# One exponential for both score tiles of a pair, in a top-32 attention and highway layer on one core

## The chip, the cores and the metric

The kernel runs on one core of one Trainium2 chip. The metric is the device time of one execution in microseconds. The core's engines are TensorE (PE, with its weight loads PEld), VectorE (DVE), ScalarE (ACT), GpSimd (POOL) and SyncE (SP), which here only issues DMAs. Each engine works through its own queue in order; what crosses from one engine to another waits on semaphores.

## The reference

```
q, k, v: (8, 8, 576, 64) f32, normal * 0.1
scores = q @ k.T / sqrt(64)
kth    = 32nd largest score of each row
attn   = exp(scores - rowmax) where scores >= kth, else 0
attn   = attn / (sum(attn) + 1e-9)
x      = (attn @ v), heads side by side: (4608, 512)
H = relu(x @ w_h);  T = sigmoid(x @ w_t + b_t)
out    = T * H + (1 - T) * x
```

## The kernel before

The work is cut into units. For each of the 8 batches there are 4 full query tiles (qt 0 to 3, 128 rows) times 8 heads, one unit each, and a rest of 64 rows (qt 4), where one unit holds two heads on the two halves of the partitions. Two units that follow each other are a pair: 18 pairs for a batch, 16 of them of full tiles, 144 pairs in all, of which 128 are of full tiles. A score tile of a unit is 128 x 576.

The main loop calls `step(i)` once for each pair, and each step works on several pairs at once. The order in which `step` writes the instructions is the order of each engine's queue (a manual schedule). In the words of one step:

- PE adds the masks of pair i to its scores in PSUM (`mask_add`, L410), then makes the attention values of pair i-3 (`values`, L494), then some filler matmuls (`spare`, L278), then the scores of pair i+2 (`scores`, L309, L318; L326 and L335 for the rest rows). After that come pieces of the layer behind the attention or of the transposes of the next batch (L522, L250).
- DVE finds candidates in the scores of pair i+1 (`segments`, 12 instructions on L353), then the largest masked scores of pair i (`below`, L420, two instructions), then goes through `refine` of pair i+1 (L366 to L382; the last one, L382, gives the row maximum and the threshold). In between it picks the kth value of pair i (`hits` L426, `pick_b` L439) and makes the masked exponentials of pair i-1 (`keep_min` L450 for the first unit, `keep_mul` L460 for the second, both on two bf16 tiles in SBUF).
- ACT makes a step function of the scores of pair i-1 (`above`, L443), evacuates one piece for the layer or the transposes, copies the values to SBUF in every second step (`xs_copy`, L508), and then does the exponential of the first unit of pair i (`expo`, L416), the copy of both score tiles of pair i+1 from PSUM (`copy_scores`, L348, one instruction of 1152 columns), possibly an evacuation of a transpose, the exponential of the second unit, and the two mask instructions of pair i+1 (`mask_count`, L397), which wait for L382.
- POOL makes the step function of the second unit (`above_one`, L454), one or two elementwise pieces of the layer (`pool_work`: L564, L610, L611, L624), multiplies hits (`pick_a`, L436), issues at most a DMA or two, and then makes the two biases (`biases`, L391) for the next step: the row maxima times -scale for the exponentials (`tb`) and the kth values times a large constant for `above` (`eb`). A dependency written by hand (`after`) holds `biases` until DVE's second masked exponential (`keep_mul`) has ended.

The masked exponentials are turned by DMA (`transposes`, L481) and multiplied with `v`, whose extra column holds a constant, so that the sum of each row comes out as a 65th column. When all 8 heads of a query tile are there, `ffn_pieces` divides by the sums (`norm`, L557, L559) and runs the layer in pieces over the next steps.

Behind the last pair `finish` does the end of the pipeline in an order of its own, and a check: ACT's Sign instructions with accumulators (`sure`, L934) count rows on which the short way is sound, and if the count is not full, a second, general pass (`tc.If(fine < 1)`) computes everything again.

Of the kernel before, what the change touches and what calls it, by code (L numbers as in the profile page):

```python
# [9 lines left out]
AF = mybir.ActivationFunctionType  # L10
ALU = mybir.AluOpType
FP32 = mybir.dt.float32
BF16 = mybir.dt.bfloat16
# [13 lines left out]
def kernel(  # L27
# [44 lines left out]
    kqpool = ctx.enter_context(tc.tile_pool(name="kq", bufs=2))  # L72
    scpool = ctx.enter_context(tc.tile_pool(name="sc", bufs=5))
    gpool = ctx.enter_context(tc.tile_pool(name="g", bufs=2))
    epool = ctx.enter_context(tc.tile_pool(name="e", bufs=4))
    cpool = ctx.enter_context(tc.tile_pool(name="c", bufs=4))
    etpool = ctx.enter_context(tc.tile_pool(name="et", bufs=6))
    xpool = ctx.enter_context(tc.tile_pool(name="x", bufs=3))
# [28 lines left out]
    for i in range(NE):  # L107
        en = consts.tile([P, 2, 2, 16], FP32, name=f"en{i}")
        nc.vector.memset(en[:, 0, :, 0:1], 3.0e38)
        ends.append(en)  # L110
    csum = consts.tile([P, NU], FP32)
    nc.vector.memset(wall[:, 0:2, KTH : KTH + 1], 0.0)

    def kth(u):
# [2 lines left out]
    def tb(u):  # L117
        return be[:, u // 2, u % 2, 0:1]
# [16 lines left out]
    vbs = []  # L135
    for i in range(2):
        vb = consts.tile([P, H, nck, DE], BF16, name=f"vb{i}")
        nc.gpsimd.memset(vb[:, :, :, D:DE], 1.0)
        vbs.append(vb)
    NEP = 4  # L140
    eps_sb = []
# [204 lines left out]
    def copy_scores(both):  # L346
        sc = scpool.tile([P, 2, S], FP32, name="sc")
        nc.scalar.copy(sc[:], both)  # L348
        return [sc[:, s, :] for s in range(2)]

    def segments(cand, sc, lo, hi):
        for s in range(lo, hi):
# [5 lines left out]
    def refine(g, cand):  # L358
# [28 lines left out]
        )  # L387
        yield

    def biases(g):  # L390
        return nc.gpsimd.tensor_tensor(be[:, g], wall[:, 2 * g : 2 * g + 2, TOP : KTH + 1 : KTH - TOP], fac[:], ALU.mult)  # L391


# [13 lines left out]
    def mask_add(ps, m1, s):  # L407
        cuts = ((0, MAIN), (MAIN, S)) if s == 0 else ((0, rem), (rem, S))
        for s0, s1 in cuts:
            nc.tensor.matmul(  # L410
                ps[:, s0:s1], ident_b[:], m1[:, s0:s1], start=False, stop=True, skip_group_check=True
            )

    def expo(u, sc):
        e = epool.tile([P, S], BF16, name="e")
        nc.scalar.activation(e[:], sc, AF.Exp, bias=tb(u), scale=scale)  # L416
        return e

    def below(u, ps):
# [19 lines left out]
        nc.vector.tensor_reduce(wall[:, pair[0] + 2 : pair[0] + 4, KTH], hit[:], mybir.AxisListType.X, ALU.add)  # L439

    def above(u, sc):
        r = epool.tile([P, S], BF16, name="r")
        nc.scalar.activation(r[:], sc, AF.Relu, bias=eb(u), scale=BIGK)  # L443
        return r

# [4 lines left out]
        return ep, nc.vector.tensor_tensor(ep[:, pad : pad + S], e[:], r[:], ALU.min)  # L450

    def above_one(u, sc):
        r = epool.tile([P, S], BF16, name="ro")
        nc.gpsimd.tensor_scalar(r[:], sc, kth(u), None, ALU.is_ge)  # L454
        return r

# [5 lines left out]
    def keep(u, sc, e):  # L462
        ep = eps_sb[u % NEP]
        pad = (u % 2) * (SP - S)
        return ep, nc.vector.scalar_tensor_tensor(
            out=ep[:, pad : pad + S],
            in0=sc,
            scalar=kth(u),
            in1=e[:],
            op0=ALU.is_ge,  # L470
            op1=ALU.mult,
        )
# [73 lines left out]

    blocks = []

    def ffn_pieces(b, qt, xs):
        nh, ng, w = shape_of(qt)  # L550
        st = dict(b=b, qt=qt, xs=xs)
        blocks.append(st)

        def norm():
            xs3 = xs[:, 0 : nh * DE].rearrange("p (h e) -> p h e", e=DE)
            rinv = cpool.tile([P, H], FP32, name="rinv")
            nc.vector.tensor_scalar(rinv[:, 0:nh], xs3[:, :, D], 1e-9, 2.0, ALU.add, ALU.mult)  # L557
            yield
            nc.vector.reciprocal(rinv[:, 0:nh], rinv[:, 0:nh])  # L559
            x = xpool.tile([P, dm], FP32, name="x")  # L560
            st["x"] = x
# [12 lines left out]

            pool_work.append((scaled, w))
            yield

        by_dma = isinstance(b, int) and units[-1][0:2] > (b, qt + 2)

        def cast():  # L580
            xb = xpool.tile([P, dm], BF16, name="xb")
            nc.gpsimd.dma_start(xb[:, 0:w], st["x"][:, 0:w])
            return partial(turn, xb)

        def turn(xb):
            st["xT"] = fpool.tile([P, n_g, P], BF16, name="xT")
            nc.sync.dma_start_transpose(st["xT"][:, 0:ng, :], xb[:, 0:w])
            flying.append(b)
            ready.extend([hh, tt])

        def xt():
            ps = fps.tile([P, 512], FP32, tag="fp", name="fp")
            for g in range(ng):
                nc.tensor.transpose(ps[:, g * P : (g + 1) * P], st["x"][:, g * P : (g + 1) * P], ident_f[:])
            xT = fpool.tile([P, n_g, P], BF16, name="xT")
            st["xT"] = xT
            psv = ps[:].rearrange("p (g j) -> p g j", j=P)
            return lambda: nc.scalar.copy(xT[:, 0:ng, :], psv[:, 0:ng, :])

        def hh():  # L600
            ps = fps.tile([P, 512], FP32, tag="fp", name="fp")
            project(ps, qt, st["xT"], wh, False)
            h2 = hpool.tile([P, dm], FP32, name="h2")
            s1 = xpool.tile([P, dm], FP32, name="s1")
            st["h2"], st["s1"] = h2, s1
            x = st["x"]

            def evac():
                nc.scalar.activation(h2[:, 0:w], ps[:, 0:w], AF.Relu)
                pool_work.append((lambda e: e.tensor_add(s1[:, 0:w], h2[:, 0:w], x[:, 0:w]), w))  # L610
                pool_work.append((lambda e: e.tensor_sub(h2[:, 0:w], h2[:, 0:w], x[:, 0:w]), w))  # L611

            return evac

        def tt():
            ps = fps.tile([P, 512], FP32, tag="fp", name="fp")
            project(ps, qt, st["xT"], wt, True)
            if by_dma:
                flying.pop()
            t = fpool.tile([P, dm], FP32, name="tt")  # L620
            h2, s1 = st["h2"], st["s1"]

            def gated(e):
# [12 lines left out]
            return evac  # L636

        return norm

    def blk_norm(k):  # L640
# [4 lines left out]
        nc.vector.tensor_scalar(rinv[:, 0:nh], xs3[:, :, D], 1e-9, 2.0, ALU.add, ALU.mult)  # L645
# [77 lines left out]
    def start_scores(g):  # L723
        b = units[pairs[g][0]][0]
        for u in pairs[g]:
            for h in units[u][2]:
                ensure_prep(b, h // 2)
        st[g] = dict(ps=scores(pairs[g], preps[b]), sc=[None, None], et=[None, None], e=[None, None])
        st[g]["seg"] = 0
        st[g]["cand"] = cands[g % len(cands)]  # L730

# [23 lines left out]
    def back_xs(g):  # L755
# [6 lines left out]
        po.clear()  # L762
        po.update(t=pso_tile(), n=0)
        if units[pairs[g][1]][2][-1] == H - 1:
            norms.append(ffn_pieces(b, qt, xs_t[b, qt]))

    late = []
    kind = [False]

    def masks_of(g):  # L770
        pr = pairs[g]
# [3 lines left out]
    def step(i):  # L775
# [40 lines left out]
            below(pr[0], st[i]["ps"][0])  # L816
            below(pr[1], st[i]["ps"][1])
        if live:
            st[i]["e"] = [expo(pr[0], st[i]["sc"][0])]
        if nxt:  # L820
            copy_both(i + 1)
        if ev:
# [10 lines left out]
                late.append(piece)  # L833
        spare(4 if late else 10)
        if live:
            st[i]["e"].append(expo(pr[1], st[i]["sc"][1]))
            pass
        ra = refine(i + 1, st[i + 1]["cand"]) if nxt else iter(())

# [83 lines left out]

    cond = consts.tile([P, NU], FP32)
    signs = consts.tile([P, NU], BF16)
    cnt = consts.tile([P, 3], FP32)
    edge = consts.tile([P, 3], FP32)
    for j, e in enumerate((-(2.0**-60), 2.0**26, -(2.0**-100))):
        nc.vector.memset(edge[:, j : j + 1], e)
    flag = consts.tile([1, 1], I32)  # L930

# [11 lines left out]
    def finish():  # L943
# [7 lines left out]
        def xs_of(qt, h0, n):  # L951
# [4 lines left out]
            return dict(b=B - 1, qt=qt, xs=xs_t[B - 1, qt])  # L956

        def masked(unit, s, of):
            return keep(unit[s], of["sc"][s], of["e"][s])
# [22 lines left out]
        mask_add(cur["ps"][1], cur["m"][1], 1)  # L982
        project(zh, z["qt"], z["xT"], wh, False)
        below(pr[1], cur["ps"][1])
        es = [expo(u, cur["sc"][s]) for s, u in enumerate(pr)]
        cur["e"] = es
        x1 = xps.tile([P, 3 * BANK], FP32, tag="x", name="xs")
        project(bank(x1, 1), z["qt"], z["xT"], wt, True)
        blk_gate(z, bank(x1, 1))
# [16 lines left out]
            nc.scalar.copy(cur["et"][s][:].rearrange("p c q -> p (c q)"), turned)  # L1006
        sure(0, wall[:, 2 : NU + 2, KTH], 1.0)
        sure(1, wall[:, 0:NU, TOP], -1.0)
        values_of(i - 1, 0)
        blk_norm(ya)  # L1010
        blk_xt(ya, bank(x1, 2))
# [22 lines left out]
        nc.vector.tensor_scalar(flag[:], po["t"][0:1, 0:1], 3.0 * P * NU - 0.5, None, ALU.is_ge)  # L1034
        blk_diff(yb, bank(x2, 0))
        return blk_out(yb)

# [101 lines left out]
```

## Time and profile before

| | |
|---|---|
| time, median of 3 runs | 806.49 us (806.15 to 808.53) |
| profiled execution, its own time | 806.17 us |
| its span in the trace | 804.5 us |
| busy: DVE | 772.8 us (96%) |
| busy: ACT | 757.2 us (94%) |
| busy: PE | 686.7 us (85%) |
| busy: POOL | 559.9 us (70%) |
| mean granted TensorE clock | 0.996 |

Busy time is the union of an engine's instructions, each with its start-up and its tail. The instructions of one engine overlap: the next one starts before the tail of the last has ended. So what an instruction costs in a full queue is the distance from its start to the start of the next one, and that is less than its duration.

### The profile page before, as it was taken

The numbers are of one execution on the slowest core, as the hardware profiler recorded it, in microseconds if no ns is written. First come the engines' busy times: TensorE is split into PE (matmuls) and PEld (weight loads), VectorE is DVE, ScalarE is ACT, GpSimd is POOL, SyncE is SP. The second block draws the span as 40 slices with busy tenths as digits, with TensorE's granted clock in tenths as the row PEclk, the third lists the DMA queues.
The fourth block names the chain that finished last, engine by engine and source line by source line (L and its number), as shares of the span: only waits on it lengthen the run. The fifth ranks groups of instructions, "written<-read, shape, count | busy, mean of one in ns | idle before, by whom it ended". The sixth has DMA issues, their size and how long they took to land.

```text
span 804.5 us, 20583 instructions
## 1 busy us (share of the span) xinstructions
PE 686.7 (85%) x6369; PEld 494.7 (61%) x6459; DVE 772.8 (96%) x4020; ACT 757.2 (94%) x1401; POOL 559.9 (70%) x712
## 2 busy tenths in 40 slices
PE   7889998888888888888987889888888888988884
PEld 5666766566666666566665666666666566665662
DVE  5999999999999999999999999999999999999996
ACT  5999999999999999999999999999999999999984
POOL 2666867777777767777767776777776777766750
PEclk9999999999999999999999999999999999999998
DMA  6789968996799667998669766898767996555653
GB/s 121 87 137 159 134 116 140 141 143 93 140 152 148 108 96 137 154 131 125 102 135 159 125 113 107 150 156 126 112 121 136 160 124 109 90 106 110 108 90 88
DMA packets 346359, 100.37 MB, mean 125 GB/s; under 512 B 330624, under 2 KB 338432, under 8 KB 346240
## 3 DMA queue, kind: packets, MB, share of 16 engines
q1 hardware_dynamic: 291024, 79.16, 54.1%
q0 software_dynamic: 53536, 19.34, 22.6%
q8 instruction: 53, 0.87, 0.4%
q10 hardware_dynamic: 1680, 0.46, 0.3%
q14 instruction: 66, 0.54, 0.2%
HBM read 31.72 MB, written 9.44 MB: 51 GB/s over the span
## 4 chain that ended last, share of the span: by engine, by line
ACT 37%; DVE 32%; PE 23%; DMA 4%; issue 3%; SPq 1%; another core or an unknown queue 0%; DVEq 0%; ACTq 0%
ACT m L397 15%; DVE wall L420 12%; DVE cand L353 9%; ACT e L416 7%; ACT sc L348 6%; PE pso L278 5%; ACT r L443 4%; PE xs L309 4%; PE xs L326 3%; DVE ep L450 3%; DMA xT<-xb 3%; PE fp L522 3%; PE xs L410 3%; PE pso L494 2%; ACT xs L508 2%
## 5 line engine op out<-in xcount | busy, mean ns | idle before, releaser
L353 DVE MAX8 cand<-xs 128x8 f32<-128x96 f32 x1728 | 297.5, 248 | 11.4 <-PE xs L335 6.2
L278 PE MATMUL pso<-cst,ident_b 128*128 128x252 bf16 x1841 | 246.8, 272 | 42.8 <-ACT xs L508 40.4
L454 POOL TENSOR_SCALAR ro<-sc,wall 128x576 bf16<-128x576 f32 x135 | 232.8, 1724 | 0.0
L416 ACT ACTIVATE e<-sc,be 128x576 bf16<-128x576 f32 x288 | 226.5, 787 | 0.1
L278 PEld LDWEIGHTS <-ident_b 128*128 128x128 bf16 x1841 | 173.4, 98 | 81.4 <-issue 49.5
L420 DVE MAX8 wall<-xs 128x8 f32<-128x576 f32 x288 | 204.3, 751 | 5.6 <-PE xs L410 3.5
L309 PE MATMUL xs<-kT,qT 64*128 64x256 f32 x1024 | 145.3, 400 | 30.6 <-DVE high L366 26.2
L348 ACT COPY sc<-xs 128x1152 f32<-128x1152 f32 x144 | 161.0, 1118 | 0.7 <-DVE cand L353 0.6
L309 PEld LDWEIGHTS xs<-kT,qT 64*128 64x128 f32 x1024 | 93.0, 186 | 61.3 <-issue 37.6
L397 ACT ACTIVATE m<-xs,wall 128x576 int8<-128x576 f32 x144 | 107.4, 746 | 18.2 <-DVE wall L382 17.1
L436 POOL TENSOR_TENSOR hit<-hit,wall 128x18 f32<-128x18 f32 x143 | 32.4, 227 | 121.2 <-DVE hit L426 114.0
L397 ACT ACTIVATE m<-sc,wall 128x576 int8<-128x576 f32 x144 | 111.4, 773 | 0.0
L443 ACT ACTIVATE r<-sc,be 128x576 bf16<-128x576 f32 x143 | 109.9, 769 | 0.0
L410 PE MATMUL xs<-m,ident_b 128*128 128x512 bf16 (+1 forms) x512 | 92.7, 274 | 17.3 <-ACT m L397 15.2
L494 PEld LDWEIGHTS <-et 128*128 128x128 bf16 (+1 forms) x1600 | 68.6, 100 | 19.2 <-issue 3.5
L391 POOL TENSOR_TENSOR be<-wall,fac 128x4 f32<-128x4 f32 x144 | 29.2, 203 | 72.5 <-DVE ep L460 53.7
L410 PEld LDWEIGHTS <-ident_b 128*128 128x128 bf16 x576 | 51.7, 97 | 44.8 <-issue 24.1
L494 PE MATMUL pso<-vb,et 128*128 128x65 bf16 (+1 forms) x1600 | 74.4, 194 | 4.2 <-DMA et<-ep 0.3
L450 DVE TENSOR_TENSOR ep<-e,r 128x576 bf16<-128x576 bf16 x143 | 64.6, 452 | 0.2 <-ACT r L443 0.2
L318 PEld LDWEIGHTS xs<-kd,qT 128*128 128x128 f32 x256 | 38.1, 188 | 42.5 <-issue 42.1
L318 PE MATMUL xs<-kd,qT 128*128 128x128 f32 x256 | 62.5, 326 | 0.0
L460 DVE TENSOR_TENSOR ep<-e,ro 128x576 bf16<-128x576 bf16 x135 | 60.7, 449 | 0.0
(127 smaller groups left out, 1028.9 us busy)
## 6 DMA issues: line engine op xcount, KB each, us to landing
kin<-in_k_dram SPq DMA_DIRECT2D x64, 128.0 KB, 2.9
qin<-in_q_dram SPq DMA_DIRECT2D x62, 128.0 KB, 3.1
out_dram<-s SPq DMA_DIRECT2D x30, 256.0 KB, 2.8
s<-h POOLq DMA_DIRECT2D x29, 256.0 KB, 4.0
et<-ep SPq DMA_TRANSPOSE x286, 3.3
xb<-x POOLq DMA_DIRECT2D x30, 128.0 KB, 3.0
vb<-in_v_dram POOLq DMA_DIRECT2D x28, 128.0 KB, 4.8
vb<-in_v_dram POOLq DMA_DIRECT2D x24, 64.0 KB, 3.1
```

Source lines behind the costliest of these rows:

```text
L278: nc.tensor.matmul(po["t"][:, 4 * DE : BANK], ident_b[:], cst[:, 0 : BANK - 4 * DE], start=True, stop=True, skip_group_check=True,)
L309: nc.tensor.matmul(ps[:, mo + n0 : mo + n0 + 256], qT[r : r + D, hp, qs : qs + P], kT[r : r + D, hp, n0 : n0 + 256], start=(n0 == 0), stop ...
L318: nc.tensor.matmul(ends, qT[:, hp, qs : qs + P], kd[:, hp, :], start=True, stop=True)
L348: nc.scalar.copy(sc[:], both)
L353: nc.vector.max(cand[:, s, :], sc[:, s * SEG : (s + 1) * SEG])
L397: nc.scalar.activation(m1[:].bitcast(I8)[:, 1 : 2 * S : 2], ps, AF.Sign, bias=wall[:, u, THR : THR + 1], scale=ABOVE, accum_out=csum[:, u ...
L410: nc.tensor.matmul(ps[:, s0:s1], ident_b[:], m1[:, s0:s1], start=False, stop=True, skip_group_check=True)
L416: nc.scalar.activation(e[:], sc, AF.Exp, bias=tb(u), scale=scale)
L420: nc.vector.max(wall[:, u, THR + 1 : KTH], ps)
L443: nc.scalar.activation(r[:], sc, AF.Relu, bias=eb(u), scale=BIGK)
L454: nc.gpsimd.tensor_scalar(r[:], sc, kth(u), None, ALU.is_ge)
L494: nc.tensor.matmul(pso[r0 : r0 + ql, col : col + DE], ets[s][:, c, gi * P2 : gi * P2 + ql], vb[:, h, vc, :], start=(c == 0), stop=(c == nc ...
```

## The change

For pairs of full tiles, ACT does one exponential over both score tiles (1152 columns) instead of two over 576. The bias of one instruction is the same for both halves of a row, so both units are measured from the larger of the two row maxima. The exponential stands where the first one stood, ahead of the copy of the next scores; the place of the second one stays empty. Pairs of the rest rows go on with two instructions, now both at the first place.

What goes with it:

- `biases` of such a pair becomes two POOL instructions: the kth value of the first unit times the constant, and the larger of two maxima times -scale. The hand-written dependency on `keep_mul` holds the one that is returned, the second.
- The small constant that is added to a sum must be in the measure of that unit. For each full query tile (32 in all) `distances` computes, on DVE, the distance of each head's own maximum to that of its pair, and on ACT the exponential of it (128 x 8). `denominators` then multiplies by it (a `scalar_tensor_tensor` in place of a `tensor_scalar`). The extra column of `v` holds 2 instead of 1, which takes the place of the factor 2.
- A fourth `sure` counts the rows whose two maxima are less than 40 apart (in the exponent); if one is not, the general pass runs.
- The tiles of the exponentials hold a pair each: 2 buffers of 1152 columns instead of 4 of 576.

```diff
-    epool = ctx.enter_context(tc.tile_pool(name="e", bufs=4))
+    epool = ctx.enter_context(tc.tile_pool(name="e", bufs=2))
...
+    dist = consts.tile([P, NU], FP32)
+    nc.gpsimd.memset(dist[:], 0.0)
...
-        nc.gpsimd.memset(vb[:, :, :, D:DE], 1.0)
+        nc.gpsimd.memset(vb[:, :, :, D:DE], 2.0)
...
-        return [sc[:, s, :] for s in range(2)]
+        return [sc[:, s, :] for s in range(2)] + [sc[:]]
...
+    def joint(g):
+        return units[pairs[g][0]][1] < nfull
+
     def biases(g):
+
+        if joint(g):
+            top = wall[:, 2 * g : 2 * g + 2, TOP]
+            nc.gpsimd.tensor_scalar(be[:, g, 0, 1:2], wall[:, 2 * g, KTH : KTH + 1], -BIGK * (1.0 - 2.0**-24), None, ALU.mult)
+            return nc.gpsimd.tensor_scalar(be[:, g, 0, 0:1], top[:, 0:1], top[:, 1:2], -scale, ALU.max, ALU.mult)
         return nc.gpsimd.tensor_tensor(be[:, g], wall[:, 2 * g : 2 * g + 2, TOP : KTH + 1 : KTH - TOP], fac[:], ALU.mult)
...
+    def expo_both(g, both):
+        e = epool.tile([P, 2, S], BF16, name="e")
+        nc.scalar.activation(e[:], both, AF.Exp, bias=be[:, g, 0, 0:1], scale=scale)
+        return [e[:, s, :] for s in range(2)]
...
+    def distances(g):
+
+        u0, u1 = pairs[g][0] + 2 - H, pairs[g][0] + 2
+        nc.vector.scalar_tensor_tensor(
+            out=dist[:, u0:u1].rearrange("p (g s) -> p g s", s=2),
+            in0=wall[:, u0:u1, TOP].rearrange("p (g s) -> p g s", s=2),
+            scalar=scale,
+            in1=be[:, g + 1 - NP : g + 1, 0, 0].unsqueeze(2).to_broadcast([P, NP, 2]),
+            op0=ALU.mult,
+            op1=ALU.add,
+        )
+        low = cpool.tile([P, H], FP32, name="share")
+        nc.scalar.activation(low[:], dist[:, u0:u1], AF.Exp)
+        return low
+
+    def denominators(rinv, sums, share):
+
+        if share is None:
+            return nc.vector.tensor_scalar(rinv, sums, 2.0e-9, None, ALU.add)
+        return nc.vector.scalar_tensor_tensor(
+            out=rinv, in0=share[:], scalar=2.0e-9, in1=sums, op0=ALU.mult, op1=ALU.add
+        )
...
-            nc.vector.tensor_scalar(rinv[:, 0:nh], xs3[:, :, D], 1e-9, 2.0, ALU.add, ALU.mult)
+            denominators(rinv[:, 0:nh], xs3[:, :, D], share)
...
         if units[pairs[g][1]][2][-1] == H - 1:
-            norms.append(ffn_pieces(b, qt, xs_t[b, qt]))
+            norms.append(ffn_pieces(b, qt, xs_t[b, qt], distances(g) if joint(g) else None))
...
+    def exponentials(g):
+        sc = st[g]["sc"]
+        return expo_both(g, sc[2]) if joint(g) else expo_each(pairs[g], sc)
...
         if live:
-            st[i]["e"] = [expo(pr[0], st[i]["sc"][0])]
+            st[i]["e"] = exponentials(i)
         if nxt:
             copy_both(i + 1)
...
         spare(4 if late else 10)
         if live:
-            st[i]["e"].append(expo(pr[1], st[i]["sc"][1]))
             pass
...
-    for j, e in enumerate((-(2.0**-60), 2.0**26, -(2.0**-100))):
+    for j, e in enumerate((-(2.0**-60), 2.0**26, -(2.0**-100), 40.0)):
...
-        es = [expo(u, cur["sc"][s]) for s, u in enumerate(pr)]
-        cur["e"] = es
+        cur["e"] = exponentials(i)
...
         sure(0, wall[:, 2 : NU + 2, KTH], 1.0)
         sure(1, wall[:, 0:NU, TOP], -1.0)
+        sure(3, dist[:], 1.0)
...
-        for j in range(3):
-            nc.tensor.matmul(po["t"][0:1, 0:1], cnt[:, j : j + 1], ones[:], start=(j == 0), stop=(j == 2))
+        for j in range(4):
+            nc.tensor.matmul(po["t"][0:1, 0:1], cnt[:, j : j + 1], ones[:], start=(j == 0), stop=(j == 3))
```

More of the change, by code (lines that the diff above doesn't have):

```diff
@@ L412, in mask_add, with expo_each @@
             )
+    def expo_both(g, both):
+        e = epool.tile([P, 2, S], BF16, name="e")
+        nc.scalar.activation(e[:], both, AF.Exp, bias=be[:, g, 0, 0:1], scale=scale)
+        return [e[:, s, :] for s in range(2)]
+    def expo_each(pair, scs):
+        e = epool.tile([P, 2, S], BF16, name="e")
+        for s, u in enumerate(pair):
+            nc.scalar.activation(e[:, s, :], scs[s], AF.Exp, bias=tb(u), scale=scale)
+        return [e[:, s, :] for s in range(2)]
+    def distances(g):
[17 more added lines that the diff above has]
+        )
     def expo(u, sc):
-        e = epool.tile([P, S], BF16, name="e")
-        nc.scalar.activation(e[:], sc, AF.Exp, bias=tb(u), scale=scale)
+        e = epool.tile([P, 2, S], BF16, name="e")[:, 0, :]
+        nc.scalar.activation(e, sc, AF.Exp, bias=tb(u), scale=scale)
         return e
@@ L441, in above @@
     def above(u, sc):
-        r = epool.tile([P, S], BF16, name="r")
+        r = epool.tile([P, S], BF16, name="r", bufs=4)
         nc.scalar.activation(r[:], sc, AF.Relu, bias=eb(u), scale=BIGK)
@@ L452, in above_one @@
     def above_one(u, sc):
-        r = epool.tile([P, S], BF16, name="ro")
+        r = epool.tile([P, S], BF16, name="ro", bufs=4)
         nc.gpsimd.tensor_scalar(r[:], sc, kth(u), None, ALU.is_ge)
@@ L468, in keep @@
             scalar=kth(u),
-            in1=e[:],
+            in1=e,
             op0=ALU.is_ge,
@@ L547, with ffn_pieces @@
     blocks = []
-    def ffn_pieces(b, qt, xs):
+    def ffn_pieces(b, qt, xs, share=None):
         nh, ng, w = shape_of(qt)
@@ L644, in blk_norm @@
         rinv = cpool.tile([P, H], FP32, name="rinv")
-        nc.vector.tensor_scalar(rinv[:, 0:nh], xs3[:, :, D], 1e-9, 2.0, ALU.add, ALU.mult)
+        denominators(rinv[:, 0:nh], xs3[:, :, D], k.get("share"))
         nc.vector.reciprocal(rinv[:, 0:nh], rinv[:, 0:nh])
@@ L727, in start_scores @@
                 ensure_prep(b, h // 2)
-        st[g] = dict(ps=scores(pairs[g], preps[b]), sc=[None, None], et=[None, None], e=[None, None])
+        st[g] = dict(ps=scores(pairs[g], preps[b]), sc=[None, None, None], et=[None, None], e=[None, None])
         st[g]["seg"] = 0
@@ L925 @@
     signs = consts.tile([P, NU], BF16)
-    cnt = consts.tile([P, 3], FP32)
-    edge = consts.tile([P, 3], FP32)
-    for j, e in enumerate((-(2.0**-60), 2.0**26, -(2.0**-100))):
+    cnt = consts.tile([P, 4], FP32)
+    edge = consts.tile([P, 4], FP32)
+    for j, e in enumerate((-(2.0**-60), 2.0**26, -(2.0**-100), 40.0)):
         nc.vector.memset(edge[:, j : j + 1], e)
@@ L955, in xs_of @@
             po["t"] = pso_tile()
-            return dict(b=B - 1, qt=qt, xs=xs_t[B - 1, qt])
+            share = distances(i - NP // 2) if qt < nfull else None
+            return dict(b=B - 1, qt=qt, xs=xs_t[B - 1, qt], share=share)
         def masked(unit, s, of):
@@ L1033, in finish @@
         blk_gate(yb, bg)
-        nc.vector.tensor_scalar(flag[:], po["t"][0:1, 0:1], 3.0 * P * NU - 0.5, None, ALU.is_ge)
+        nc.vector.tensor_scalar(flag[:], po["t"][0:1, 0:1], 4.0 * P * NU - 0.5, None, ALU.is_ge)
         blk_diff(yb, bank(x2, 0))
```

## The prediction

> **What bounds the kernel now.** I read the page first: how busy each engine is, and which work the chain that ended last went through.
>
> ```profile
> PE 686.7 (85%) x6369; PEld 494.7 (61%) x6459; DVE 772.8 (96%) x4020; ACT 757.2 (94%) x1401; POOL 559.9 (70%) x712
> ACT 37%; DVE 32%; PE 23%; DMA 4%; issue 3%; SPq 1%; another core or an unknown queue 0%; DVEq 0%; ACTq 0%
> ```
>
> DVE and ACT are both nearly full, and the chain changes engine all the time, so neither line says what ACT's time is worth. For that I read who waits for whom, DVE's own waits and ACT's longest:
>
> ```profile
> DVE cand L353 <- PE xs L335: 6.2, 15, 0.5
> DVE wall L420 <- PE xs L410: 3.5, 8, 1.3
> DVE cand L353 <- PE xs L318: 3.4, 10, 0.6
> ACT m L397 <- DVE wall L382: 17.1, 47, 1.0
> ```
>
> DVE's three longest waits of the steady part come to 13.1 us. They are for PE: twice for scores, once for masks that are added. None names ACT. ACT waits longer, for DVE. So I followed one turn of the loop in the chain, over two steps in the middle:
>
> ```profile
> 533.27 2.48 DMA xT<-xb
> ...
> 540.78 1.59 ACT m L397 x4
> 542.37 0.67 ACT r L443
> 543.03 0.47 ACT kT L251
> 543.50 0.29 ACT xs L508
> ...
> 543.83 1.02 PE pso L278 x8
> 544.85 1.06 PE xs L309 x8
> 545.92 0.43 PE xs L318 x2
> ...
> 546.37 2.02 DVE cand L353 x12
> ...
> 548.44 1.43 DVE wall L420 x2
> 549.87 0.10 DVE high L366
> ...
> 551.21 0.13 DVE wall L382
> ...
> 551.36 1.59 ACT m L397 x4
> ...
> 554.37 0.67 ACT e L416
> ```
>
> From one m behind L382 (540.78) to the next but one (551.36) are 10.58 us for two steps. ACT stands in this loop with the masks, `above`, one evacuation and the copy of the values. The exponentials don't stand in it: they come behind the copy of the values. ACT's row of the same time shows where they are:
>
> ```profile
> 548.64 0.79 ACT L416 ACTIVATE e<-sc,be 128x576 bf16<-128x576 f32 x1
> 549.31 1.13 ACT L348 COPY sc<-xs 128x1152 f32<-128x1152 f32 x1
> 550.31 0.80 ACT L416 ACTIVATE e<-sc,be 128x576 bf16<-128x576 f32 x1
> 551.36 0.74 ACT L397 ACTIVATE m<-xs,wall 128x576 int8<-128x576 f32 x1 [0.25 <-DVE wall L382]
> ```
>
> Behind the second exponential ACT waits 0.25 us for DVE. A shorter exponential here makes that wait longer and nothing else.
>
> **ACT's side.** Start to start an exponential takes 0.67 us (548.64 to 549.31), so two are 1.34. One of 1152 columns is bounded by 1.34 (no fixed part) and by 1.00, the copy of as many columns (549.31 to 550.31). Its slope comes from another ACT instruction with a bias in SBUF:
>
> ```profile
> L934 ACT ACTIVATE signs<-cond,edge x1: 548/548/548, 791.6 to 791.6; 128x288 bf16<-128x288 f32 x1
> ```
>
> From 548 ns for 288 columns to 790 for 576 are 0.84 ns a column; 576 more make 0.67 + 0.48 = 1.15. That saves 0.19 a pair, 128 x 0.19 = 24 us of ACT (0 to 44). I take little of it for the time: of the 3.5 us that DVE waits for masks a part comes from ACT being behind, a part from layer pieces that wait for a transpose DMA (533.27 lies ahead of such a wait). **Taken: -1.5**, bounds 0 and -13.1, all three waits.
>
> The copy of the next scores starts later by 1.15 - 0.67 = 0.48 us, with the evacuation behind it. The scores themselves are held by DVE's L420, so this stays covered; where ACT's wait for L382 is gone, it costs nothing either, because the masks come 0.19 earlier than before. The new exponential of 128 x 8 follows the copy of the values in 32 steps, at most 0.55 us (the 548 row), about 0.19 start to start; that eats what the pair saves in this step, no more.
>
> **DVE's side.** 32 `distances`. Small DVE instructions of the chain take 0.10 us (L366 at 549.87), the upper bound is twice that with a wait for operands, the lower zero. They stand between `keep_mul` and the candidates of a step, where DVE sometimes waits anyhow:
>
> ```profile
> 545.80 0.45 DVE L460 TENSOR_TENSOR ep<-e,ro 128x576 bf16<-128x576 bf16 x1
> ...
> 551.24 0.45 DVE L460 TENSOR_TENSOR ep<-e,ro 128x576 bf16<-128x576 bf16 x1
> 551.61 2.08 DVE L353 MAX8 cand<-xs 128x8 f32<-128x96 f32 x12
> ```
>
> Behind the second L460 the candidates start after 0.37 us, behind the first after 0.57 (546.37 in the chain), because the scores end at 546.35: 0.2 us free in every second step. So I count half: 32 x 0.10 / 2, and 0.3 for `denominators`, whose instruction reads a second operand. **Taken: +1.9** (0 to 6.4).
>
> **POOL's side**, where the change costs most. In these rows, the first and the last of 39 steps that I found alike (144 pairs gone through), DVE and POOL meet:
>
> ```profile
> 79.99 1.26 POOL L610 TENSOR_TENSOR s<-h,x 128x512 f32<-128x512 f32 x1
> 80.72 0.60 DVE L366 TENSOR_TENSOR high<-cand 128x48 f32<-128x48 f32 x1
> ...
> 767.39 1.27 POOL L611 TENSOR_TENSOR h<-h,x 128x512 f32<-128x512 f32 x1
> 768.69 0.19 DVE L366 TENSOR_TENSOR high<-cand 128x48 f32<-128x48 f32 x1
> ```
>
> L366 reads two operands from SBUF. At 80.72 POOL's piece ran until 81.25, and L366 took 0.60 us, until just behind it, in place of 0.19. At 768.69 POOL ended at 768.66, and L366 wasn't held: the margin was 0.03. The other way round:
>
> ```profile
> L391 POOL TENSOR_TENSOR be<-wall,fac x144: 188/193/711, 13.8 to 782.7; 128x4 f32<-128x4 f32 x144
> 781.79 1.53 DVE L465 SCALAR_TENSOR_TENSOR ep<-sc,wall,e 128x576 bf16<-128x576 f32 x2
> 782.68 0.71 POOL L391 TENSOR_TENSOR be<-wall,fac 128x4 f32<-128x4 f32 x1 [1.64 <-DVE ep L465]
> ```
>
> The 711 ns bias lies under a DVE instruction with two SBUF operands and ends just behind it, at 783.39 against 783.32. So each waits for what the other has running. [...]
>
> POOL's queue behind `keep_mul`:
>
> ```profile
> 498.31 0.20 POOL L391 TENSOR_TENSOR be<-wall,fac 128x4 f32<-128x4 f32 x1 [1.28 <-DVE ep L460]
> 498.48 1.72 POOL L454 TENSOR_SCALAR ro<-sc,wall 128x576 bf16<-128x576 f32 x1
> ```
>
> One more small instruction moves all behind it by 0.17 us (498.31 to 498.48), and the piece that ends ahead of L366 with it. A lower bound is 0, where the kth instruction, which isn't tied to `keep_mul`, runs earlier. An upper one comes from L454: at 2.1 ns a column (L610: 1.27 less 0.19, over 508) 576 columns make 1.22 of its 1.72, which leaves 0.50 for one such instruction with a scalar operand. For each step I added the shift to POOL's end and counted how far L366 is pushed: 0.18 us gives 39 steps and 3.3 us together, 0.10 gives 1.1, 0.50 gives 24. About half of them lie in steps with those 0.2 us free, and half of that is given back. **Taken: +2.4** (0.8 to 17). I am nearest to the small price, because L391's own row is the closest in size.
>
> In 22 steps POOL has issued no DMA and sits idle ahead of L391 (1.28 us at 498.31). There the kth instruction is released by `pick_b`, under L450, runs once that ends, and holds L460 by up to 0.17: 3.7 us at most, half given back. **Taken: +1.6** (0 to 3.7). In the other steps POOL comes out of a DMA issue while L460 runs, and has to wait for its end.
>
> **The end.** From the chain:
>
> ```profile
> 789.24 0.82 ACT signs L934 x2
> ...
> 790.98 0.25 ACT xT L659
> ...
> 791.35 0.39 ACT xs L508
> ```
>
> The two Signs stand in ACT's queue ahead of the cast and the copy that the last block waits for. A third one over 288 columns adds about 0.6 (548 ns plus its accumulator read, less the overlap), the last small exponential 0.2. **Taken: +0.8** (0.4 to 1.2).
>
> Sum: -1.5 + 1.9 + 2.4 + 1.6 + 0.8 = +5.2. The profiled execution took 806.17 us, the median of the runs is 806.49; I leave these 0.3 us aside. Forecast **811.4 us**.
>
> **The rivals.**
>
> *ACT sets the pace after all (faster).* For it: ACT's 37% of the chain, and stretches like the one from 554.37 on, where the chain runs on through ACT's exponentials and the copy. Against it: the loop above and 17.1 us of ACT waiting for L382. If ACT being late causes half of DVE's 13.1 us and POOL's shift stays free, 806.2 - 6.5 + 1.9 + 0.8 = 802.4. [...] Together 0.12.
>
> *Nothing moves.* The shifts fall into DVE's waits for scores, the end costs its 0.8: 807, within 0.3% (2.4 us, about what a measurement of this kernel can tell from no change). For it: the 0.2 us in every second step. Against it: 39 steps with a margin under 0.07, half of them in steps without such a wait. 0.14.
>
> *POOL becomes the bound.* Small POOL instructions with scalar operands cost 0.50 instead of 0.17. Then the loop POOL, L366, L460, POOL is longer than DVE's own in most steps: 806.2 + 17 + 1.9 + 1.6 + 0.8 - 1.5 = 826. For it: L454's long time. Against it: L391's 193 ns. From a shift of about 0.3 it decides. 0.09.
>
> That the general pass runs is no rival: q and k are normal numbers times 0.1, so maxima of rows lie far less than 40 apart.
>
> The forecast has 0.65.
>
> **How the numbers follow.** Faster 0.12 is the first rival, same 0.14 the second, slower 0.74 the forecast and POOL as the bound. The forecast's own range, with POOL's shift between 0.10 and 0.30 and the rest at its bounds, is about 807 to 819. For 8 in 10 I reach down through most of "nothing moves" and up into POOL's case: 804.3 to 822.
>
> **What the profile afterwards would show.** ACT's busy time falls by 20 to 25 us, exponentials of 1152 columns take about 1.27, and ACT's wait for L382 grows from 17 towards 35 us or more: that is where its gain goes. L366 keeps its minimum of 0.19, but its mean rises, and stretched ones end with POOL's pieces. DVE's busy time rises by some 5 us, since a held instruction counts as busy. I would be wrong if ACT's wait for L382 stays at 17 us while the span falls (ACT was the pace), if L366 isn't stretched more often (POOL's shift is covered), or if the POOL instructions of L391 take far from 0.2 us.

## The result, and the profile after

The changed kernel takes 816.31 us (median of 4 runs, 815.83 to 819.25) against 807.51 us (4 runs, 806.15 to 809.87) for the kernel before. The ratio is 1.0113 [1.0077, 1.0149], so the change costs about 9 us. (The ratio comes from all runs and isn't quite the quotient of the two medians.) The profiled execution took 815.83 us, its span is 814.2 us.

First the busy times of the changed kernel, and its chain by engine:

```profile
PE 697.4 (86%) x6461; PEld 494.8 (61%) x6461; DVE 781.9 (96%) x4053; ACT 739.9 (91%) x1307; POOL 614.5 (75%) x841
DVE 45%; ACT 30%; PE 19%; issue 2%; DMA 2%; SPq 0%; POOL 0%; DVEq 0%; ACTq 0%; POOLq 0%
```

ACT has 17.3 us less to do, DVE 9.1 us more, POOL 54.6 us more. (PE's rows can't be compared: the trace of before lacks some 90 PE records.) The chain has moved from ACT to DVE.

ACT's row of the steady part shows that the new exponential is as fast as was forecast:

```profile
540.00 0.22 ACT L447 ACTIVATE share<-dist 128x8 f32<-128x8 f32 x1
540.11 1.25 ACT L426 ACTIVATE e<-sc,be 128x1152 bf16<-128x1152 f32 x1
541.25 1.12 ACT L350 COPY sc<-xs 128x1152 f32<-128x1152 f32 x1
...
545.16 1.25 ACT L426 ACTIVATE e<-sc,be 128x1152 bf16<-128x1152 f32 x1
546.31 1.11 ACT L350 COPY sc<-xs 128x1152 f32<-128x1152 f32 x1
547.81 0.74 ACT L407 ACTIVATE m<-xs,wall 128x576 int8<-128x576 f32 x1 [0.40 <-DVE wall L384]
```

From its start to the start of the copy are 1.15 us (545.16 to 546.31), against twice 0.67 for two. ACT is done sooner, and then waits 0.40 us for L384, which is the old L382. The small exponential of the distances takes 0.11 us, start to start. The waits of the whole kernel, DVE's three and ACT's:

```profile
ACT m L407 <- DVE wall L384: 43.2, 89, 1.5
...
DVE cand L355 <- PE xs L337: 5.8, 15, 0.5
...
DVE wall L464 <- PE xs L420: 4.0, 6, 1.5
...
DVE cand L355 <- PE xs L320: 3.3, 8, 0.8
```

ACT's wait for DVE has grown from 17.1 to 43.2 us. DVE's three waits for PE come to 13.1 us, exactly what they came to before. What ACT gave up doesn't show in them.

Where DVE's time went shows in the groups by line, here the first instruction of `refine` with two operands in SBUF (L366 before, L368 after); the columns behind the bar are busy time, mean ns of one, and idle time ahead. Before:

```profile
L366 DVE TENSOR_TENSOR high<-cand 128x48 f32<-128x48 f32 x144 | 29.0, 201 | 0.0
```

After:

```profile
L368 DVE TENSOR_TENSOR high<-cand 128x48 f32<-128x48 f32 x144 | 37.5, 260 | 0.0
```

It is the same instruction with 8.5 us more. What stretches it is found where the timelines of POOL and DVE are laid side by side. POOL:

```profile
534.61 1.26 POOL L655 TENSOR_TENSOR h<-h,x 128x512 f32<-128x512 f32 x1
...
536.74 0.97 POOL L189 DMA_DIRECT2D vb<-in_v_dram  x1 [0.29 <-issue]
537.79 0.24 POOL L399 TENSOR_SCALAR be<-wall 128x1 f32<-128x1 f32 x1
538.12 0.30 POOL L400 TENSOR_SCALAR be<-wall 128x1 f32<-128x1 f32 x1
538.39 1.75 POOL L498 TENSOR_SCALAR ro<-sc,wall 128x576 bf16<-128x576 f32 x1
...
541.95 0.63 POOL L626 DMA_DIRECT2D xb<-x  x1 [0.29 <-POOL hit L480]
542.66 0.36 POOL L399 TENSOR_SCALAR be<-wall 128x1 f32<-128x1 f32 x1
543.12 0.30 POOL L400 TENSOR_SCALAR be<-wall 128x1 f32<-128x1 f32 x1
543.39 1.75 POOL L498 TENSOR_SCALAR ro<-sc,wall 128x576 bf16<-128x576 f32 x1
```

DVE:

```profile
535.10 0.85 DVE L368 TENSOR_TENSOR high<-cand 128x48 f32<-128x48 f32 x1
535.86 0.19 DVE L370 TENSOR_TENSOR low<-cand 128x48 f32<-128x48 f32 x1
...
537.21 0.45 DVE L504 TENSOR_TENSOR ep<-e,ro 128x576 bf16<-128x576 bf16 x1
537.57 0.16 DVE L438 SCALAR_TENSOR_TENSOR dist<-wall,be 128x8 f32<-128x8 f32 x1
...
542.49 0.45 DVE L504 TENSOR_TENSOR ep<-e,ro 128x576 bf16<-128x576 bf16 x1
```

POOL's layer piece of 534.61 ends at 535.87. L368 starts at 535.10 and ends just behind it, at 535.95: 0.85 us for what takes 0.19. Over all steps its time beyond 0.195 us adds up to 10.3 us, where the kernel before has 1.6. In 43 steps it takes more than 0.21 us, before in 8, and each of the 43 starts under a piece of POOL's and ends 0.06 to 0.07 us behind it.

POOL is later because of its two bias instructions. From the end of `keep_mul` (L504: 537.21 + 0.45 = 537.66) to POOL's step function (538.39) are 0.73 us in the first of these steps; in the second (542.94 to 543.39) they are 0.45. Worked out in the same way for all steps of full tiles, the kernel before has a median of 0.27 us and also 0.27 at the upper quartile; the changed one has 0.45 and 0.70. Both cases stand in these rows. At 537.71 a DMA issue ends just behind `keep_mul`, and both bias instructions follow. At 542.58 one ends ahead of it: L399 starts under L504 (542.66), ends just behind it (543.02), and only L400 follows. L399 starts under L504 in 55 of its 128 steps. The instructions themselves, with minimum, median and maximum in ns:

```profile
L399 POOL TENSOR_SCALAR be<-wall x128: 222/248/678, 3.4 to 778.7; 128x1 f32<-128x1 f32 x128
...
L400 POOL TENSOR_SCALAR be<-wall x128: 291/296/303, 13.4 to 779.7; 128x1 f32<-128x1 f32 x128
```

### The profile page after: what moved, and what is told of

Read it like the earlier page. It is cut to its first block, busy times and chain, and to the rows that moved or that the text cites. A ratio compares the mean times of both kernels' runs of the same rounds, so it can differ in the third digit from the quotient of the medians.

```text
span 814.2 us, 20745 instructions
## 1 busy us (share of the span) xinstructions
PE 697.4 (86%) x6461; PEld 494.8 (61%) x6461; DVE 781.9 (96%) x4053; ACT 739.9 (91%) x1307; POOL 614.5 (75%) x841
## 4 chain that ended last, share of the span: by engine, by line
DVE 45%; ACT 30%; PE 19%; issue 2%; DMA 2%; SPq 0%; POOL 0%; DVEq 0%; ACTq 0%; POOLq 0%
DVE wall L464 15%; ACT m L407 14%; DVE cand L355 11%; DVE ep L494 5%; PE pso L280 4%; ACT r L487 4%; ACT sc L350 4%; ACT e L426 4%; PE xs L420 3%; PE xs L311 2%; PE xs L328 2%; DMA xT<-xb 2%; PE fp L566 2%; DVE high L368 2%; DVE en L375 2%
## 5 line engine op out<-in xcount | busy, mean ns | idle before, releaser
L498 POOL TENSOR_SCALAR ro<-sc,wall 128x576 bf16<-128x576 f32 x135 | 235.4, 1744 | 0.0
L426 ACT ACTIVATE e<-sc,be 128x1152 bf16<-128x1152 f32 x128 | 160.5, 1254 | 0.1
L407 ACT ACTIVATE m<-xs,wall 128x576 int8<-128x576 f32 x144 | 107.2, 744 | 44.6 <-DVE wall L384 43.2
L420 PE MATMUL xs<-m,ident_b 128*128 128x512 bf16 (+1 forms) x576 | 106.4, 285 | 20.4 <-ACT m L407 18.2
L480 POOL TENSOR_TENSOR hit<-hit,wall 128x18 f32<-128x18 f32 x143 | 32.0, 224 | 94.5 <-DVE hit L470 89.7
L494 DVE TENSOR_TENSOR ep<-e,r 128x576 bf16<-128x576 bf16 x143 | 64.5, 451 | 0.6 <-ACT sc L350 0.2
L400 POOL TENSOR_SCALAR be<-wall 128x1 f32<-128x1 f32 x128 | 38.0, 297 | 30.9 <-DVE wall L384 9.7
L504 DVE TENSOR_TENSOR ep<-e,ro 128x576 bf16<-128x576 bf16 x135 | 60.5, 448 | 0.0
```

What stands on the lines that cost most here:

```text
L407: nc.scalar.activation(m1[:].bitcast(I8)[:, 1 : 2 * S : 2], ps, AF.Sign, bias=wall[:, u, THR : THR + 1], scale=ABOVE, accum_out=csum[:, u ...
L420: nc.tensor.matmul(ps[:, s0:s1], ident_b[:], m1[:, s0:s1], start=False, stop=True, skip_group_check=True)
L426: nc.scalar.activation(e[:], both, AF.Exp, bias=be[:, g, 0, 0:1], scale=scale)
```

## Experiments

The theory after the result: the loss is POOL's, whose layer piece now ends under L368; the shorter exponential is worth nothing, because ACT waits for DVE anyway. Rivals: the new exponential hurts by its place (the second unit's scores are no longer spread over the step, the copy comes later); or the added work on DVE, ACT and at the end makes the loss. Each time below is a median, each ratio is against the kernel before on the same chip.

**One bias instruction, as before (e1).** From the changed kernel, without the added block in `biases`. All else stays, with the exponential's bias taken from the first unit's own maximum in place of the larger one.

```diff
     def biases(g):
-        if joint(g):
-            top = wall[:, 2 * g : 2 * g + 2, TOP]
-            nc.gpsimd.tensor_scalar(be[:, g, 0, 1:2], ...)
-            return nc.gpsimd.tensor_scalar(be[:, g, 0, 0:1], top[:, 0:1], top[:, 1:2], -scale, ALU.max, ALU.mult)
         return nc.gpsimd.tensor_tensor(be[:, g], ...)
```

> The change with one POOL instruction for the biases, as before (all pairs; the single exponential is then measured from the first unit's maximum in place of the larger one). Theory 1 (the second POOL instruction pushes POOL's piece into DVE's L368): the stretched L368 fall back from 10.1 us in all to about 1.6, and the time to about 808 to 809; what stays above the kernel before is the end (about 0.8) and the small DVE instructions (1 to 2). Rival A (the later copy of the next scores, behind the long exponential, holds PE and DVE): nothing comes back, 815 to 817. Rival B (the small DVE and ACT instructions for the distances cost it): at most 1 us comes back, 815.

**Two exponentials at their old places (e2).** The changed kernel with its two bias instructions, but ACT's instructions as before.

```diff
-            st[i]["e"] = exponentials(i)
+            st[i]["e"] = [expo_one(i, 0)]
...
+            st[i]["e"].append(expo_one(i, 1))
             pass
```

> The change with two exponentials in their old places, both from the larger maximum; POOL, the distances and the fourth Sign stay as in the change. Theory 1 (ACT is not the pace, POOL is): the time stays where the change has it or rises by 0 to 3 us, 816 to 819, and ACT's wait for L384 falls back from 43 us towards 20. Rival A (the later copy costs): down to about 809. If the one exponential had gained its 24 us in secret, with POOL's loss on top of it, this would go to about 830 to 840.

**ACT's part alone (e3).** e1 without `distances`, without the small exponential and without the fourth Sign: the kernel before with one exponential in place of two.

```diff
-            norms.append(ffn_pieces(b, qt, xs_t[b, qt], distances(g) if joint(g) else None))
+            norms.append(ffn_pieces(b, qt, xs_t[b, qt], None))
...
-        sure(3, dist[:], 1.0)
```

> The one exponential alone: one POOL instruction for the biases, exponentials from the first unit's maximum, no distances, no fourth Sign; the constant that is added to a sum is not scaled. Theory 1: ACT's saving alone, 0 to 1.5 us below the kernel before, 805 to 807, with 24 us less busy ACT and ACT waiting for L384 some 40 us. Rival C (ACT does set the pace in part, and the gain was eaten by POOL): 800 to 803. Rival A: above the kernel before by 5 us or more.

**A shorter step function on POOL (e4).** The whole change, both bias instructions too, but POOL computes the second unit's step function over 288 of 576 columns, and `keep_mul` uses it for both halves. So the second half of that mask isn't computed.

```diff
-        nc.gpsimd.tensor_scalar(r[:], sc, kth(u), None, ALU.is_ge)
+        nc.gpsimd.tensor_scalar(r[:, 0 : S // 2], sc[:, 0 : S // 2], kth(u), None, ALU.is_ge)
```

> The change with POOL's step function of the second unit (L498) over 288 of the 576 columns, used for both halves: it leaves half of that mask uncomputed and takes 0.8 us a step off POOL, while both bias instructions stay. Theory 1 (it is POOL's end that meets L368): the stretched L368 vanish, 808 to 810. If the bias instructions cost by themselves, for instance by holding the masked exponentials or by their waits, and not through POOL's end: 815 to 817 still.

Measured side by side, with the kernel before at 807.6 us:

| | us | ratio |
|---|---|---|
| e1, one bias instruction | 810.41 | 1.0036 [1.0023, 1.0050] |
| e2, two exponentials | 816.98 | 1.0118 [1.0100, 1.0137] |
| e3, ACT's part alone | 807.88 | 1.0003 [0.9995, 1.0012] |
| e4, shorter step function | 809.81 | 1.0030 [1.0019, 1.0041] |

L368 in e1, in e2, in e3 and in e4, each by the groups of its own trace:

```profile
L368 DVE TENSOR_TENSOR high<-cand 128x48 f32<-128x48 f32 x144 | 29.4, 204 | 0.0
```

```profile
L368 DVE TENSOR_TENSOR high<-cand 128x48 f32<-128x48 f32 x144 | 38.6, 268 | 0.0
```

```profile
L368 DVE TENSOR_TENSOR high<-cand 128x48 f32<-128x48 f32 x144 | 29.2, 203 | 0.0
```

```profile
L368 DVE TENSOR_TENSOR high<-cand 128x48 f32<-128x48 f32 x144 | 28.6, 199 | 0.0
```

With one bias instruction 5.9 us of the loss are gone (816.31 to 810.41), and L368 is back at 204 ns (201 before). With both bias instructions and a shorter POOL queue (e4) the same is gone, and `keep_mul` itself takes 450 ns there (448 in the change), so it isn't a shorter `keep_mul` that pays. With two exponentials (e2) the loss is all there, L368 stretched as in the change: one exponential or two makes no difference that the intervals can tell, and ACT's wait for L384 falls from 43.2 to 21.6 us. And one exponential without the rest (e3) gives the time of before within 0.12%. So the pair of bias instructions makes two thirds of the loss, by way of POOL's later end, and the rival of the exponential's place falls. A wait for a late result of POOL isn't the way: in the lists of waits, before and after, no other engine waits for a POOL instruction of the loop. The other rival holds for the remaining third, e1 less e3, 2.5 us: the distances and the end. (These are differences of medians; e1's and e3's intervals are 1 us to either side, the change's own 3 us. e2 less e1, which has the same difference in POOL, gives 6.6.) Of the expectations, those of e2 and e4 were met; e1 came out 1.4 us above its 808 to 809, and e3 0.9 above its 805 to 807, without the small gain that was hoped for. No run has the pair of bias instructions without the distances, so whether the two add up or help each other stays open.

Where the gain of e3 went, by ACT's wait for DVE in e3:

```profile
ACT m L402 <- DVE wall L384: 37.2, 77, 2.0
```

From 17.1 to 37.2: 20.1 us, and ACT's busy time in e3 is 20.0 us less than before (737.2 against 757.2). All of it has become waiting.

**POOL's part alone (e5).** The kernel before with one more small POOL instruction behind the biases, into a scratch column; only the new one is held behind `keep_mul`.

```diff
-        return nc.gpsimd.tensor_tensor(be[:, g], ...)
+        nc.gpsimd.tensor_tensor(be[:, g], ...)
+        top = wall[:, 2 * g : 2 * g + 2, TOP]
+        return nc.gpsimd.tensor_scalar(spot[:, g : g + 1], top[:, 0:1], top[:, 1:2], -scale, ALU.max, ALU.mult)
```

> The kernel before with one more small POOL instruction behind the biases (the larger of two maxima times -scale, as in the change, into a place that nobody reads), held behind keep_mul like the biases; two exponentials, no distances. Theory 1: POOL's shift of 0.27 us a step alone does it; L366 is stretched by some 9 to 11 us in all instead of 1.6, and the time rises by 5 to 8 us, to 813 to 816. If the change's loss needs the single exponential or the distances as well: 807 to 809.

809.60 us against 807.67, ratio 1.0022 [1.0013, 1.0031]: slower, by less than expected: it lies 3.4 us under the 813 to 816 of theory 1, and nearer to the 807 to 809 of its rival. Its group of that instruction, and POOL's timeline:

```profile
L367 DVE TENSOR_TENSOR high<-cand 128x48 f32<-128x48 f32 x144 | 32.8, 228 | 0.0
```

```profile
533.76 0.21 POOL L392 TENSOR_TENSOR be<-wall,fac 128x4 f32<-128x4 f32 x1
533.94 0.31 POOL L394 TENSOR_SCALAR spot<-wall 128x1 f32<-128x1 f32 x1
534.23 1.74 POOL L457 TENSOR_SCALAR ro<-sc,wall 128x576 bf16<-128x576 f32 x1
```

The added delay was smaller than meant, which fits the small loss. The old bias, no longer held, costs its short 0.18 us (533.76 to 533.94) where the changed kernel's kth instruction takes 0.33 (537.79 to 538.12), and often runs ahead. The step function starts 0.40 us behind `keep_mul` in the median, 0.13 later than before, where the change has 0.18 more and a longer tail. By rows the relation is the same in kind: 3.6 us more of stretch beyond 0.195 us (5.2 against 1.6) make 1.9 us, in the change 8.7 make 5.9. That the rest of the change isn't needed for the loss is so far argued, not shown: e2 does without the single exponential, but no run does without the distances.

**Can the freed ACT time be used? (e6, e7).** ACT stands in the loop with an evacuation ahead of the copy of the values. If the copy goes first, the loop has less of ACT in it. e6 is e3 with this order, e7 is the kernel before with it.

```diff
-        if late:
-            late.pop(0)()
         if back:
             back_pv(j)
             back_xs(j)
             st.pop(j)
+        if late:
+            late.pop(0)()
```

> The one exponential alone (as in e3_act_only), and the copy of the values now stands ahead of the evacuation of the layer's piece in ACT's queue, not behind it. If the loop is as read in the prediction (masks, above, evacuation, copy of the values, PE's filler and scores, DVE), the copy starts some 0.2 us earlier in most second steps, and 64 of them give up to 12 us, less where DVE itself is full: 798 to 804. If the loop is misread: 807 to 809, as e3.

> The kernel before, two exponentials, with the same move of the copy of the values. If ACT then becomes the pace, because its step of 5.2 us without a wait is longer than what is left of the loop, this stays near 805 to 807 and e6 is 2 us or more below it: the one exponential pays once the loop is shorter. If ACT is still not the pace: as e6.

e6 took 809.91 us (1.0019 [1.0007, 1.0031]) and e7 816.44 us (1.0105 [1.0091, 1.0120]), with 807.67 for the kernel before. Both expectations of a gain failed: e6 lies 6 us above its 798 to 804, e7 9 us above its 805 to 807. That e6 would lie 2 us or more below e7 did come true. ACT's waits in e6, and its timeline in a step that shows why:

```profile
ACT m L402 <- DVE wall L384: 24.4, 58, 1.8
...
ACT xs L547 <- PE pso L533: 17.2, 26, 1.5
```

```profile
588.42 0.77 ACT L482 ACTIVATE r<-sc,be 128x576 bf16<-128x576 f32 x1
590.21 0.38 ACT L547 COPY xs<-pso 128x260 f32<-128x260 f32 x1 [1.03 <-PE pso L533]
590.49 0.60 ACT L672 ACTIVATE tt<-fp 128x512 f32<-128x512 f32 x1
```

Two regular steps in the middle of a batch shorten from 10.49 to 10.40 us (medians over the batches). But in two steps of a batch the values come late, and ACT stands idle ahead of its copy while the evacuation, ready, waits behind it: in the seventeenth 1.03 us, in e3's order 0.55. By the medians the step behind the seventeenth takes 5.51 us in place of 5.19. So what the loop gains, these steps give back.

What e7 is good for is the comparison: in this order two exponentials cost 6.5 us more than one. ACT's waits and PE's wait for ACT's masks, in e7:

```profile
PE xs L410 <- ACT m L397: 25.4, 79, 1.2
ACT xs L508 <- PE pso L494: 15.4, 24, 1.5
ACT m L397 <- DVE wall L382: 10.9, 28, 1.0
```

ACT waits only 10.9 us for L382, so there is little left to hide ACT's 20 us behind. PE's wait for ACT's masks is 25.4 us, against 15.2 before and 21.1 in e6.

**A cheaper check (e8), and the order only where it fits (e9, e10).** e8 is e6 with a sound condition for one exponential that costs nothing in the steps: once, at the end, POOL squares the differences of the pairs' maxima, and a Sign behind the others counts them. e9 is e8, and e10 is e7, with the old order in steps 2 and 16 of each batch.

```diff
+        nc.gpsimd.tensor_tensor(far[:], wall[:, 0:NU:2, TOP], wall[:, 1:NU:2, TOP], ALU.subtract)
+        nc.gpsimd.tensor_tensor(far[:], far[:], far[:], ALU.mult)
...
+        sure(3, far[:], -1.0)
```

```diff
+        if late and k_in in (2, 16):
+            late.pop(0)()
         if back:
...
-        if late:
+        if late and k_in not in (2, 16):
             late.pop(0)()
```

> As e6, with a sound check for the shared measure: in place of the distances per query tile, POOL squares the difference of a pair's maxima once at the end, and a fourth Sign, placed where ACT waits in the tail, counts those less than 2 apart in the exponent (then the unscaled constant is off by less than a factor of 8 at 1e-9). Theory: within 0.7 us of e6.

> e8_both_checked, but the copy of the values stays behind the evacuation in the third and the seventeenth step of each batch, where PE's values come late and ACT stood 0.6 and 1.0 us idle ahead of the copy in e6. If that idle time is what ate the gain (0.3 us in the step behind each seventeenth, 8 times): 2 to 4 us below e8, 805 to 807, equal to the kernel before or up to 0.3% below it. If the gain of the other steps isn't there: 808 to 809.

> The kernel before with two exponentials and the same restricted move. ACT has 0.19 us a step less to spare: some 6 us above e9, 811 to 814, if what e6 against e7 showed (6.5 us for the one exponential once the copy stands first) comes from all steps; near e9 if it came from the two places taken out here.

e8: 809.21 us, 1.0014 [1.0003, 1.0026] (before 807.67). Beside e9 and e10 the kernel before took 806.82 us. e9: 806.16 us, 1.0000 [0.9986, 1.0013]. e10: 811.58 us, 1.0066 [1.0051, 1.0081]. All three came out where they were expected. ACT's waits in e9, then in e10:

```profile
ACT m L401 <- DVE wall L383: 27.2, 59, 1.2
...
ACT xs L531 <- PE pso L517: 9.3, 21, 1.0
```

```profile
ACT m L397 <- DVE wall L382: 11.6, 32, 1.0
...
ACT xs L508 <- PE pso L494: 7.9, 21, 0.8
```

By the ratios, leaving the two steps out takes 3.1 us off e7 and 1.1 off e8; the second is inside the intervals. One exponential is worth 5.4 us here again (e10 less e9). With two exponentials the new order still costs 4.8 us (e10 against before), and PE's wait for ACT's masks is still 22.9 us. But the best version only equals the kernel before: none of the ten beats it. Whether another order of ACT's work would turn the 27.2 us that e9 still waits into time stays open.

## Why the prediction was right, and where it was not

It said slower, 811.4 us in a range of 804.3 to 822.0, by the mechanism that the runs show. The measured 816.31 lies 4.9 us above: 1.3 is the base (806.2 against 807.51), and 3.6 the sum. By its terms:

| term | taken | measured | from |
|---|---|---|---|
| ACT's shorter exponential | -1.5 | 0 (+0.3, inside its interval) | e3 |
| distances and denominators, and the end | +1.9 and +0.8 | +2.5 together | e1 less e3 |
| POOL's shift | +2.4 | +5.9 | change less e1 |
| kth instruction ahead of `keep_mul` | +1.6 | in the same 5.9; 0 at L460, now L504 | change less e1 |

*ACT.* The size of the instruction was right (1.15 us start to start, 1.254 in duration for a forecast of 1.27), and so was where the gain would go. The busy time fell by 17.3 us, a little less than the 20 to 25 forecast, since the small exponentials and the fourth Sign take some 3 us of it back (740.2 us in e1, 737.2 in e3). The failed step is "of the 3.5 us that DVE waits for masks a part comes from ACT being behind". That wait is 4.0 us in the change and 4.2 in e3, where ACT's part stands alone. None of it was ACT's to give.

*Distances and the end.* Forecast 2.7, measured 2.5. By the traces of one execution each, the steps of the 32 blocks became longer by 0.06 to 0.07 us in the median, about 2 us together, and the end by 0.6 to 0.7. In detail the counting by half was too kind: a distance takes 0.08 us start to start (537.57 to the candidates at 537.65), less than the 0.10 taken, but all of it is paid. The end by its chain, where the Sign's accumulator stands ahead of the cast and the copy:

```profile
796.84 0.23 ACT share L447
...
800.46 0.19 ACT signs L981
800.64 0.47 ACT xT L703
801.11 0.29 ACT xs L552
```

*POOL.* The mechanism and the place hold. 39 steps were to be hit, and 43 are stretched where 8 were, but that these two lie so near is partly luck: with the prediction's count redone from the trace of before (40 steps), 24 of the 43 are among the steps it marks, with 7.6 of the 10.3 us. The size was wrong. The failed step is "One more small instruction moves all behind it by 0.17 us", with the price of L391. The two instructions that came are of another form, and it is dearer: on one column 0.23 us with a constant (the median of L399 where it starts under neither masked exponential; 0.25 of all) and 0.30 with a column as scalar operand (L400), against 0.193 for four columns of two tensors. And the kth instruction often doesn't run ahead of time: in 55 of 128 steps it starts under L504. Where POOL comes out of a DMA issue while L504 runs, it is held until that ends (L399 at 542.66: 0.36 us; the prediction saw this hold, "has to wait for its end", and counted no shift for it); where the issue ends later still, both instructions stand behind L504. So the shift is 0.18 in the median but 0.43 at the upper quartile and 0.32 in the mean, and the stretch of L368 rose by 8.7 us where 3.3 were counted. That a quarter is given back was near: 5.9 of 8.7 stayed.

*The kth term.* It was to hold L460 by up to 0.17 us in 22 steps. From L384 to the next `keep_mul` are 0.12 us in the change as before (537.09 to 537.21; the medians agree too), and `keep_mul` keeps its 0.45 us. L399 does start under the first masked exponential (L494) in 20 steps, near the 22 counted, and in 18 of them it ends 0.08 to 0.09 us behind it. But L504 starts 0.04 to 0.11 us behind L494 as it did before, and isn't stretched; why this short overlap costs it nothing stays open. The term is zero at that place; its instruction is paid in POOL's shift instead. That it was counted at all brought the sum nearer to the time, which is luck. So the sum was short by 3.6 us (8.8 by the medians, against 5.2): 1.9 by both POOL terms together (4.0 against 5.9), 1.5 by ACT's term and 0.4 by which e3 lies above 807.51 (0.3 above its own 807.6, inside its interval); the distances and the end go 0.2 the other way.

*The rivals.* "ACT sets the pace" is refuted for this order by e3 and e2, which differ from before and from the change by nothing measurable. Something of the same rival holds in the order of e7 and e10, where ACT's wait for L382 is down to 10.9 and 11.6 us and the exponential is worth 6.5 and 5.4. "Nothing moves" came true of ACT's part alone (e3), not of the whole change. "POOL becomes the bound" lay nearer than its 0.09 says: its price of 0.50 us wasn't met, but the shift is over 0.30 us, where it was to begin to decide, in 51 of 115 steps of full tiles. POOL isn't the bound for that: in the change it still waits 89.7 us for DVE's `hits` (L470), and has 0% of the chain.

Each of the two engines was seen to wait for the other. In the change L368 at 535.10 took 0.85 us in place of 0.19 and ended just behind POOL's piece (535.95 against 535.87). L399 took 0.68 us at most, at 763.43, in place of 0.23, and ended 0.09 us behind a masked exponential (L509, which started at 763.21 and took 0.81 us). Why the two hold each other isn't shown by these runs.

## What to carry to other kernels

An engine that is 94% busy may still wait for another engine again and again (here 47 times), and then a shorter instruction on it can bring nothing: read what ends its waits, and what work stands in the loop, before shortening it. A small instruction added on an engine that is 70% busy can cost more than the large saving brings, if its queue ends within some hundredths of a microsecond of the start of an instruction on another engine that was seen to be stretched where the two overlap (here L368, 0.85 us in place of 0.19); count the steps with such a margin, and take the price from a row of the same form, not of the same size (here 0.23 and 0.30 us were paid where a row of another form had 0.193). When a saving vanishes, look for the order in which it would count, and measure it there with and without.

## What the runs showed of the hardware

On POOL, a `tensor_scalar` on 128 x 1 took longer in the change (248 ns in the median of all L399, 232 where neither masked exponential held it; 296 for L400) than a `tensor_tensor` on 128 x 4 before (L391, 193 ns). Where L399, on one column, started under one of the two masked exponentials of VectorE (L494, L504; two bf16 tiles in SBUF, 128 x 576), it ended 0.08 us behind it or later: so in all 75 steps in which it did. At 542.66 it took 0.36 us and ended at 543.02, 0.08 behind L504's end.
